# Twenty operations get another rank in a planned instruction order: linear attention, then a token-and-channel mixing block, on one core

## The chip, the cores and the metric

The kernel runs on one core of a Trainium2 chip. The metric is device time in microseconds (us): 360.75 us is the median of three runs of the kernel before, 360.08 the lowest and 361.04 the highest. The core has a matrix engine (TensorE, "PE" in the profile, with "PEld" for its weight loads), a vector engine (VectorE, "DVE"), a scalar engine (ScalarE, "ACT"), GpSimd ("POOL") and SyncE ("SP"), which issues most transfers. TensorE writes into PSUM, which has eight banks.

## The reference

Eight batches, eight heads, 576 rows, head size 64; the model width is 8 x 64 = 512 and the hidden width 2048.

```python
kv  = einsum('bhsd,bhse->bhde', k, v)            # no softmax: k and v are multiplied first
out = einsum('bhsd,bhde->bhse', q, kv)
out = out / sqrt(mean(out*out, -1) + 1e-6) * g_norm
x   = out as [batch, 576, 512]
a1  = alpha1 * x + beta1
u   = x + lam * einsum('ts,bsd->btd', w_tok, a1)  # mixes tokens
a2  = alpha2 * u + beta2
y   = u + lam * (relu(a2 @ w_ch1) @ w_ch2)        # mixes channels, two layers
```

## The kernel before

The kernel is written as a list of operations. Each call `P.op(engine, cost, function, r=..., w=...)` adds one: the engine that runs it (or a choice of two), a cost estimated in microseconds, what it reads and writes, and a function that emits its instructions. An operation has a number, `idx`, its place in that list. One operation can be many instructions: the product of line 893 for four chunks is 64 matmul instructions in the trace.

Work goes batch by batch, in chunks of 128 rows; chunks 0 to 3 cover rows 0 to 511, and "the tail" is the last 64 rows. For batch 0 the parts are these: the product k'v (line 694); q transposed by TensorE (line 723, two pairs of heads for each half of the heads, and line 737 for the tail); q times kv (line 893); its square on ACT (line 927), a sum on VectorE (line 929), a root (line 932) and a reciprocal (line 935), and the scaling (line 948); w_tok transposed (line 1452, five groups, and line 1466 for the tail columns), with ACT or VectorE copying each group out of PSUM, and summed (line 1488); token mixing (line 1134 for batch 0, line 1057 for batch 1, line 1088 for the tails of both batches), and the VectorE add of its result (lines 1151, 1070 and 1096); a transpose of u (line 1169) with a copy that scales it (lines 1178 and 1179); the first layer (lines 1235 and 1247 for the first four groups, 1220 for the others, sixteen groups `fj` of 128 hidden channels) with relu on ACT (line 1210); the second layer (line 1311), sixteen parts of four matmuls for batch 0, part n of chunk c adding hidden channels 4n to 4n+3 of sixteen, with a VectorE add (line 1321) after the last part of a chunk.

While batch 0 is in its layers, batch 1 is prepared: q is split into a high and a low half-precision part (copies that the trace shows at lines 564 and 565, subtraction at line 649), transposed by TensorE (line 672), multiplied by kv (line 881, with 459 for the second matmul of each pair), squared and scaled as before. Casts of the first-layer weights (trace lines 564 and 565) and scaling of the second-layer weights (line 1543) also run there.

The order on each engine is not the order of the list. `schedule` plays the program through in microseconds of its own: whenever an engine is free, it takes the operation of lowest rank `pri` that is ready, which means that what it needs is done and that a PSUM bank is free for its result. TensorE looks at the first sixteen operations of its queue. While the first layer of batch 0 has not begun and nothing is ready for TensorE, a filler matmul on zeros (line 1624) is put in. The result is a fixed order for each engine, written into the program with semaphores.

`plan` sets the ranks. It takes the operations on which the first layer and second layer of batch 0 and the first group of batch 1 depend, gives each a latest start worked backwards from due times, runs `schedule` eight times, and keeps the ranks of the best. A rank is about a planned start in microseconds, minus 1000. Operations that none of those need, such as everything later in batch 2 and onward, keep their number in the list as rank. The function `shake` adds random numbers to ranks for each seed, and the call passes no seeds:

```python
        for seed in seeds:
            kept_pri = shake(kept_pri, seed)
        run(kept_pri)
        ...
        P.plan(due, 8, ())
```

Of the kernel before, what the change touches and what calls it, by code (L numbers as in the profile page):

```python
# [2 lines left out]

# [46 lines left out]
class Prog:  # L50
# [72 lines left out]
                o.pri = -1000.0 - way  # L123
        return rank

    def plan(self, due, rounds, seeds):

        kept = [(o, o.eng, o.cost, set(o.deps)) for o in self.ops]
        tiles = {t: list(t.ops) for o in self.ops for t in o.tiles}
        ahead = sorted(self.hasten(due), key=lambda o: o.idx)  # L130
        movable = [o for o in ahead if o.eng != "SP"]

        def run(pri):
            self.ops[:] = [o for o, *_ in kept]
            for o, eng, cost, deps in kept:
                o.eng, o.cost, o.deps = eng, cost, set(deps)
                o.start = o.end = None
            for t, ops in tiles.items():
                t.bank, t.ops = None, list(ops)
            self.warm[3].bank, self.warm[3].ops = None, []  # L140
            self.lastw.pop(self.warm[3], None)
            for o in movable:
                o.pri = pri[o]
            for o in self.first:
                o.pri = -3000.0
            self.schedule()
            return max(o.end for o in self.ops)

        def backward():
            late, free, users = {}, {}, {}  # L150
            for o in ahead:
                for y in o.deps:
                    users.setdefault(y, []).append(o)
            base = max(o.start - d for o, d in due.items())
            for o, d in due.items():
                late[o] = base + d
            for o in sorted(ahead, key=lambda o: -o.end):
                if o in late:
                    continue
                by = min([late[u] for u in users.get(o, ()) if u in late] or [base])  # L160
                by -= o.end - o.start - o.cost
                if o.lat is None:
                    by = min(by, free.get(o.eng, 1e9))
                late[o] = by - o.cost
                if o.lat is None:
                    free[o.eng] = late[o]
            return {o: late[o] - 1000.0 for o in movable}

        def shake(pri, seed):
            rnd = random.Random(seed)  # L170
            share, by = (0.02, 0.1, 0.3)[seed % 3], (1.0, 3.0)[seed % 2]
            return {o: pri[o] + (rnd.gauss(0.0, by) if rnd.random() < share else 0.0)
                    for o in movable}

        pri = {o: o.pri for o in movable}
        best, kept_pri = None, None
        for i in range(rounds):
            last = run(pri)
            if best is None or last < best - 1e-6:
                best, kept_pri = last, pri  # L180
            pri = backward()
        for seed in seeds:
            kept_pri = shake(kept_pri, seed)
        run(kept_pri)

    def schedule(self):
        queues = {}
# [277 lines left out]
def bass_transnormer_attn__then__resmlp_affine_kernel(  # L465
# [15 lines left out]
    with ExitStack() as stack:  # L481
        P = Prog(nc, stack)
# [1016 lines left out]
        def run(gens):  # L1499
            for gen in gens:  # L1500
                for f in gen:
                    f()
# [47 lines left out]
        due = {}  # L1550
# [74 lines left out]
                            start=True, stop=True)  # L1625
        P.warm = (next(iter(due)), warm, ["wz"], P.ptile(1))
        P.first = [wz_op]
        P.plan(due, 8, ())
        P.synchronize()
        P.emit()  # L1630

# [27 lines left out]
```

## Time and profile before

| | |
|---|---|
| median of three runs | 360.75 us (360.08 to 361.04) |
| span of the profiled execution | 357.9 us |
| the profiled execution's own time | not listed beside the span; the median is 2.85 us above it |
| TensorE busy | 348.7 us, 97% |
| VectorE busy | 236.6 us, 66% |
| ScalarE busy | 158.9 us, 44% |
| GpSimd busy | 20.2 us, 6% |
| moved by DMA | 60.17 MB, 168 GB/s on average |

A timeline row gives the start, the length of a merged run of instructions, the engine, the line, what was written from what, and in brackets the idle time of the engine just before, with what ended it. In the view by stretch, "PE busy (x)" is the busy time of TensorE in that stretch with the number of its instructions. The span counts from the first instruction to the last; the runs' time also has what lies around it.

### The profile page before, as it was taken

Reading aid. Unit: us, or ns where it says so; the run is one execution under the profiler, and the core shown is the slowest. Engines: PE = TensorE matmul, PEld = TensorE weight load, DVE = VectorE, ACT = ScalarE, POOL = GpSimd, SP = SyncE. Lnnn points to the kernel's source line nnn. Section 1 sums busy time; section 2 is a strip of 40 time slices with the busy share of each in tenths; the row PEclk is TensorE's granted clock in tenths of the full one; section 3 lists DMA queues with packets and bytes.
Section 4 is the critical chain, followed back from the end, with each engine's and each line's share of the span. In section 5 each row is a group of like instructions: output and inputs, shape, how many; then the busy total and the mean of one; then the engine's idle time right before and its main releaser. Section 6 shows DMA issues by size and latency. Waiting matters only on the chain.

```text
span 357.9 us, 7888 instructions
## 1 busy us (share of the span) xinstructions
PE 348.7 (97%) x3570; PEld 204.3 (57%) x3387; DVE 236.6 (66%) x347; ACT 158.9 (44%) x270; POOL 20.2 (6%) x29
## 2 busy tenths in 40 slices
PE   8999999999999999999999999999999999999996
PEld 7778554477644544467644554457654554457644
DVE  3478899778993389947884388956885369920021
ACT  2556983068800494028810396017930185007600
POOL 4152004300000000000000000000000000000000
PEclk9999999999999999999999999999999999999999
DMA  8999999499156930599256840486036400240022
GB/s 280 350 363 377 406 408 371 173 178 338 59 134 188 291 141 3 117 186 336 100 117 181 268 185 2 101 178 194 3 83 153 116 6 0 55 132 6 2 59 88
DMA packets 79897, 60.17 MB, mean 168 GB/s; under 512 B 53037, under 2 KB 63541, under 8 KB 79736
## 3 DMA queue, kind: packets, MB, share of 16 engines
q1 hardware_dynamic: 79840, 59.67, 54.7%
q8 instruction: 27, 0.44, 0.5%
q14 instruction: 6, 0.05, 0.0%
q10 hardware_dynamic: 24, 0.01, 0.0%
HBM read 38.82 MB, written 9.44 MB: 135 GB/s over the span
## 4 chain that ended last, share of the span: by engine, by line
PE 94%; ACT 4%; issue 1%; DVE 0%
PE ps L1311 34%; PE ps L1262 20%; PE ps L1220 13%; PE ps L1057 7%; PE ps L694 5%; PE ps L1624 2%; PE ps L881 2%; PE ps L459 2%; ACT ht L1210 2%; PE ps L1088 1%; PE ps L1134 1%; PE ps L723 1%; PE ps L1292 1%; PE ps L1169 1%; PE ps L1109 1%
## 5 line engine op out<-in xcount | busy, mean ns | idle before, releaser
L1311 PE MATMUL ps<-w,ht 128*128 128x512 bf16 x537 | 121.8, 379 | 2.2 <-issue 1.4
L1209 ACT ACTIVATE ht<-ps,hb 128x512 bf16<-128x512 f32 (+1 forms) x96 | 71.0, 740 | 43.1 <-PE ps L1262 31.9
L1311 PEld LDWEIGHTS ps<-w,ht 128*128 128x128 bf16 x560 | 53.5, 98 | 63.7 <-issue 2.0
L1262 PE MATMUL ps<-a2t,w 128*128 128x320 bf16 (+1 forms) x512 | 72.7, 299 | 0.0
L1262 PEld LDWEIGHTS ps<-a2t,w 128*128 128x128 bf16 x512 | 49.4, 98 | 20.4
L1220 PE MATMUL ps<-a2t,w 128*128 128x512 bf16 x231 | 53.1, 379 | 1.0 <-issue 0.7
L758 ACT ACTIVATE kvd<-ps 64x128 bf16<-64x128 f32 x24 | 6.5, 272 | 96.0 <-PE ps L694 95.9
L1321 DVE TENSOR_TENSOR xm<-ps,xm 128x512 f32<-128x512 f32 x31 | 20.8, 687 | 29.7 <-PE ps L1311 29.6
L1220 PEld LDWEIGHTS ps<-a2t,w 128*128 128x128 bf16 x240 | 22.7, 98 | 26.1 <-issue 0.5
L929 DVE TENSOR_REDUCE small<-sq 128x16 f32<-128x1024 f32 (+1 forms) x18 | 20.2, 1126 | 16.6 <-ACT sq L927 16.6
L1057 PE MATMUL ps<-rt,wt 128*128 128x512 bf16 x107 | 25.1, 379 | 0.3
L1210 ACT ACTIVATE ht<-ps 128x512 bf16<-128x512 f32 (+1 forms) x32 | 19.9, 665 | 1.3 <-DVE hb L565 0.6
L763 DVE TENSOR_TENSOR kvd<-ps,kvd 64x128 bf16<-64x128 f32 x24 | 6.9, 289 | 20.4 <-ACT kvd L758 20.0
L948 DVE TENSOR_TENSOR xm<-ps,small 128x1024 f32<-128x1024 f32 x16 | 19.6, 1224 | 0.5
L1070 DVE TENSOR_TENSOR xm<-ps,xm 128x1024 f32<-128x1024 f32 x14 | 17.1, 1222 | 4.2 <-PE ps L1109 2.6
L927 ACT ACTIVATE sq<-ps 128x1024 f32<-128x1024 f32 (+1 forms) x18 | 17.0, 951 | 6.0 <-PE ps L893 4.0
L694 PEld LDWEIGHTS ps<-vf,kf 64*64 64x64 f32 x1008 | 16.0, 135 | 5.6 <-issue 4.4
L694 PE MATMUL ps<-vf,kf 64*64 64x64 f32 x1008 | 17.9, 221 | 0.6 <-ACT a2t L1178 0.6
L1057 PEld LDWEIGHTS ps<-rt,wt 128*128 128x128 bf16 x112 | 10.9, 98 | 12.9 <-issue 0.4
L1321 DVE TENSOR_TENSOR xtl<-ps,xtl 128x512 f32<-128x512 f32 x4 | 2.8, 692 | 21.2 <-PE ps L1311 21.1
L649 DVE TENSOR_TENSOR qs<-qf,qs 128x1024 bf16<-128x1024 f32 x14 | 16.7, 1215 | 0.1
L1076 DVE TENSOR_TENSOR a2b<-xm,a_bc 128x512 bf16<-128x512 f32 x24 | 15.5, 688 | 0.4
(130 smaller groups left out, 337.0 us busy)
## 6 DMA issues: line engine op xcount, KB each, us to landing
out_dram<-xm SPq DMA_DIRECT2D x31, 256.0 KB, 2.7
qf<-in_q_dram SPq DMA_DIRECT2D x7, 1024.0 KB, 6.8
kf<-in_k_dram SPq DMA_DIRECT2D x6, 1152.0 KB
vf<-in_v_dram SPq DMA_DIRECT2D x6, 1152.0 KB, 10.0
stg<-in_moe_w_ch_dram SPq DMA_DIRECT2D x3, 1024.0 KB, 13.7
kf<-in_moe_w_ch_dram SPq DMA_DIRECT2D x2, 1024.0 KB
kf<-in_k_dram SPq DMA_DIRECT2D x2, 576.0 KB, 5.1
vf<-in_v_dram SPq DMA_DIRECT2D x2, 576.0 KB, 6.3
```

Of the source, the lines that this page charges most:

```text
L694: m = e.matmul(t.ap(slice(64 * x, 64 * x + 64))[:, y, 0:64], nine(kf, b, a)[r, x, c, :], nine(vf, b, a)[r, x, c, :], start=(c == 0), stop= ...
L927: P.op("ACT", act_us(64 * m), lambda e: e.activation(split(sqv) if b == 0 else sqv, raw(), ACT.Square), r=[t], w=[("sq", sqs)])
L929: P.op("DVE", dve_us(64 * m), lambda e: e.tensor_reduce(out=smv, in_=sqv.rearrange("p (h d) -> p h d", h=m), axis=AX.X, op=ALU.add), r=[(" ...
L948: P.op("DVE", dve_us(64 * m), lambda e: e.tensor_tensor(out=x3, in0=raw() if b == 0 else split(raw()), in1=inv, op=ALU.mult), r=[t, ("sm", ...
L1057: m = e.matmul(t.ap()[:, i, :], tok_w(sc, c), rsrc(b, sc), start=(sc == 0), stop=(sc == 4))
L1070: P.op("DVE", dve_us(512 * n), lambda e: e.tensor_tensor(out=x, in0=t.ap(rows) if n > 1 else t.flat(rows), in1=x, op=ALU.add), r=[t] + xk, ...
L1209: o = P.op("ACT", act_us(n) + 0.07 * (b > 1), lambda e: e.activation(dst, src(), ACT.Relu, bias=hb[:, fj:fj + 1]) if b > 1 else e.activati ...
L1210: dst, src(), ACT.Relu, bias=hb[:, fj:fj + 1]) if b > 1 else e.activation(
L1220: m = e.matmul(t.flat(), w, a2t[:, dj, 0:512], start=(dj == 0), stop=(dj == 3))
L1262: m = e.matmul(t.ap()[:, i, 0:n], w1[:, dj, 128 * fj:128 * fj + 128], a2t[:, dj, 320 * i:320 * i + n], start=(dj == 0), stop=(dj == 3))
L1311: m = e.matmul(t.flat(), ht[:, fj, 128 * c:128 * c + 128], w2[:, fj, :], start=(fj == 0), stop=(fj == 15))
L1321: P.op("DVE", dve_us(512), lambda e: e.tensor_tensor(out=x, in0=t.flat(), in1=x, op=ALU.add), r=[t] + keys, w=keys)
```

## The change

The third argument of `plan` is now a table of moves, from an operation's number to a value in microseconds that is added to its rank before the last call of `schedule`. A negative value ranks the operation earlier, a positive one later. `shake` goes, which was never called.

```diff
-    def plan(self, due, rounds, seeds):
+    def plan(self, due, rounds, moves):
...
-        for seed in seeds:
-            kept_pri = shake(kept_pri, seed)
-        run(kept_pri)
+        run({o: kept_pri[o] + moves.get(o.idx, 0.0) for o in movable})
...
-        P.plan(due, 8, ())
+        P.plan(due, 8, {
+            52: -8.5, 56: -7.8, 68: 2.6, 129: 7.7, 154: 4, 158: 13.5, 159: 5.2, 162: 11.6,
+            169: 3.2, 204: -2.1, 205: -10.7, 237: 13.4, 246: 2.9, 254: 13.8, 258: 7, 273: 20,
+            276: 8.5, 278: 8.6, 283: 88.2, 298: -5.6})
```

Counting the calls of `P.op` gives what the numbers stand for:

| number | move | operation (line in the trace, engine) |
|---|---|---|
| 52 | -8.5 | batch 0, q of the second half of the heads transposed, first pair (723, TensorE) |
| 56 | -7.8 | batch 0, q tail of the second half transposed (737, TensorE) |
| 68 | +2.6 | tail columns of w_tok transposed (1466, TensorE) |
| 129 | +7.7 | cast of a piece of the first-layer weights (564 or 565) |
| 154 | +4 | batch 1, high part of q, chunks 0 and 1 (564 or 565) |
| 158, 159 | +13.5, +5.2 | batch 1, high part and low part of q, tail (564 or 565; 649) |
| 162 | +11.6 | batch 1, q of chunks 2 and 3, first half of the heads, transposed (672, TensorE) |
| 169 | +3.2 | batch 1, copy of the transposed q, chunks 2 and 3, second half (564 or 565) |
| 204 | -2.1 | batch 1, q times kv, chunks 0 and 1 (881, TensorE) |
| 205 | -10.7 | its square (927, ACT) |
| 237 | +13.4 | batch 1, reciprocal for the tail (1006, VectorE) |
| 246, 254, 258 | +2.9, +13.8, +7 | batch 0, first layer, groups 6, 10 and 12 (1220, TensorE) |
| 273 | +20 | batch 1, token mixing of chunk 2 (1057, TensorE) |
| 276 | +8.5 | token mixing of the tails of batches 0 and 1 (1088, TensorE) |
| 278, 283 | +8.6, +88.2 | batch 0, second layer, chunk 0 part 0 and chunk 1 part 1 (1311, TensorE) |
| 298 | -5.6 | batch 1, first transpose of u (1169, TensorE) |

Since `schedule` plays all engines through together, an operation that is not in the table can change its place too.

More of the change, by code (lines that the diff above doesn't have):

```diff
@@ L1 @@
-import random
 from contextlib import ExitStack
@@ L167, in backward @@
             return {o: late[o] - 1000.0 for o in movable}
[L169 to L173, printed above, removed]
         pri = {o: o.pri for o in movable}
```

## The prediction

> **What bounds the kernel now.** I read the page's busy table first, then the clock row, then busy time by stretch, then the PE timeline of the first 77 us, because every moved operation lies in there.
>
> ```profile
> span 357.9 us, 7888 instructions
> PE 348.7 (97%) x3570; PEld 204.3 (57%) x3387; DVE 236.6 (66%) x347; ACT 158.9 (44%) x270; POOL 20.2 (6%) x29
> ...
> PEclk9999999999999999999999999999999999999999
> ```
>
> ```profile
> core 0: us, PE busy (x) PEld busy (x) DVE busy (x) ACT busy (x) POOL busy (x), PEclk, DMA share, GB/s
> 6.00:26.00 20.00, 19.23 (x419) 15.14 (x421) 12.56 (x24) 10.17 (x22) 5.30 (x8) 1.00 1.06 359
> 26.00:52.00 26.00, 25.84 (x305) 17.32 (x276) 22.46 (x31) 20.81 (x35) 3.44 (x5) 1.00 1.06 396
> 52.00:71.50 19.50, 19.39 (x96) 8.72 (x95) 16.94 (x21) 4.73 (x8) 7.66 (x5) 1.00 0.79 285
> 71.50:77.00 5.50, 4.93 (x166) 4.35 (x165) 5.28 (x8) 3.66 (x9) 0.00 (x0) 1.00 0.80 180
> ```
>
> TensorE is busy 97% of the span at a granted clock of 1.00, so the time is the sum of what TensorE does plus its holes. The change keeps the same operations, so the useful matmuls cannot get shorter; only holes can go or come. The stretches have holes of 20.00 − 19.23 = 0.77, 26.00 − 25.84 = 0.16, 19.50 − 19.39 = 0.11 and 5.50 − 4.93 = 0.57 us: 1.61 us in all. Some of that is not real: a matmul record can be missing. Two more holes are hidden inside the busy time, namely filler matmuls of zeros (line 1624) that the planner puts in wherever TensorE has nothing ready before the first layer of batch 0 begins.
>
> ```profile
> 14.10 1.97 PE L723 MATMUL ps<-ident,qf 128*64 128x128 f32 x32
> 16.00 0.33 PE L737 MATMUL ps<-ident,qft 64*128 64x64 f32 x2
> 16.11 0.60 ACT L564 ACTIVATE qt<-ps 128x512 f32<-128x512 f32 x1
> 16.26 0.55 PEld L1624 LDWEIGHTS ps<-a2b 128*128 128x128 bf16 x4
> 16.37 0.29 DVE L565 COPY qt<-ps 128x128 f32<-128x128 f32 x1
> 17.23 0.44 PE L893 MATMUL ps<-kvd,qt 64*64 64x64 f32 x7
> 18.06 1.17 PE L893 MATMUL ps<-kvd,qt 64*64 64x64 f32 x65 [0.39 <-issue]
> 19.16 0.75 PE L1466 MATMUL ps<-ident,ht 64*128 64x64 f32 x5
> 19.84 1.23 PE L1452 MATMUL ps<-ident,ht 128*128 128x128 f32 x8
> 20.62 1.18 ACT L564 ACTIVATE wt<-ps 128x512 bf16<-128x512 f32 x3
> 20.78 0.43 PEld L1624 LDWEIGHTS ps<-a2b 128*128 128x128 bf16 x3
> 21.55 1.55 PE L1452 MATMUL ps<-ident,ht 128*128 128x128 f32 x12
> 22.22 1.55 ACT L564 ACTIVATE wt<-ps 128x512 bf16<-128x512 f32 x3
> 22.93 1.47 PE L1134 MATMUL ps<-rt,wt 128*128 128x256 bf16 x12
> 24.24 1.70 PE L1488 MATMUL ps<-wt,sel 128*128 128x512 bf16 x10
> ```
>
> The weight loads count the fillers: four from 16.26 and three from 20.78. Between them stands a hole of 0.39 us that no engine ended ("issue"), before line 893. The last hole is the only one with a named releaser:
>
> ```profile
> 52.11 12.90 PE L1311 MATMUL ps<-w,ht 128*128 128x512 bf16 x58
> 64.94 1.05 PE L1088 MATMUL ps<-rt,wt 128*64 128x512 bf16 x8
> ...
> 69.39 1.03 PE L1311 MATMUL ps<-w,ht 128*128 128x512 bf16 x4
> 70.25 1.03 PE L1057 MATMUL ps<-rt,wt 128*128 128x512 bf16 x4
> ...
> 71.33 0.60 PE L1169 MATMUL ps<-ident,xtl 128*128 128x128 f32 x4
> 71.53 1.23 DVE L1070 TENSOR_TENSOR xm<-ps,xm 128x1024 f32<-128x1024 f32 x1
> 71.64 1.50 ACT L1178 ACTIVATE a2t<-ps,ab 128x128 bf16<-128x128 f32 x4 [9.18 <-PE ps L1169]
> 72.50 1.28 PE L694 MATMUL ps<-vf,kf 64*64 64x64 f32 x72 [0.57 <-ACT a2t L1178]
> 73.80 0.69 DVE L1321 TENSOR_TENSOR xm<-ps,xm 128x512 f32<-128x512 f32 x1
> ```
>
> The kv product of batch 2 (line 694) needs two neighbouring banks of PSUM and has to wait until ACT empties some of the four small transposes (line 1169). One wide matmul lasts (64.94 − 52.11) / 60 = 0.214 us; sixty stand for fifteen second-layer parts of four, of which two records are missing. So the three fillers at 20.78 are worth 0.64 us and the four at 16.26 are worth 0.86.
>
> **The ceiling.** The moved operations come at 14 us and later. What they can at most take away is 0.86 + 0.39 + 0.64 + 0.57 = 2.46 us. After 77 us nothing is moved by hand, and the order there starts from the same state, somewhat earlier.
>
> **The change, part by part.** *Operations 52 and 56.* Operation 52 (line 723, q of the second half) cannot start before its data have landed. In the trace it already follows the kv product without a hole, so its new rank changes nothing: 0. Operation 56 (line 737) now goes before the second pair of line 723 instead of behind it. That delays this pair by 0.27 us (16.27 − 16.00) and its copy on ACT from 16.71 to about 16.98, while the small product that needs the tail can run where fillers ran. The large product of line 893, however, starts at 18.06 behind the "issue" hole, more than a microsecond behind that copy. I read the hole as instructions that had not yet been fetched, since all 16 DMA engines are busy (share 1.06) and no semaphore is named. Then fewer fillers ahead of it only lengthen the hole: 0, between −0.86 − 0.39 (hole and fillers go) and +0.27 (the delayed pair reaches the product). I take 0, as the row nearest to it is the one at 18.06. If the hole is a wait that moves with the product instead, at least its 0.39 us goes as well, and the forecast below becomes 359.1; that is part of the rival in which more goes. The Trainium skill, page "Runtime: NRT & Kernel Launch", section "Instruction fetch mechanics", speaks for this second reading: it holds that fetching the next block is mostly hidden behind the issue of the current one. This trace shows the hole, without a cause.
>
> *Operation 68* (line 1466, tails of the w_tok transposes) goes behind three of the five transposes of line 1452. In the trace it is first; then come two groups of line 1452, and then TensorE runs out: three fillers until ACT's copies (from 20.62) return a bank. With the tail later, the two banks of the small product of line 893 come back sooner as well, because its chain on ACT and DVE started earlier. So the fillers go: −0.64. The bounds are 0 (the banks return no sooner, since ACT's three copies run back to back until 21.80) and −0.64. Whatever is late next is line 1488 at 24.24, which needs ACT's last copy of w_tok; that ends at 22.22 + 1.55 = 23.77, 0.47 us ahead of it, and token mixing of chunks that are ready (line 1134) can fill the rest, so I let all of the gain pass.
>
> *Operations 129, 154, 158, 159, 162, 169, 204, 205 and the first-layer groups 246, 254, 258.* They sit in a stretch with 0.16 us of holes, so there is nothing to win there. Here is what it could lose:
>
> ```profile
> 34.74 0.63 ACT L564 ACTIVATE qs<-qft 64x512 bf16<-64x512 f32 x1
> ...
> 38.74 6.21 PE L1220 MATMUL ps<-a2t,w 128*128 128x512 bf16 x27
> ...
> 41.40 1.04 ACT L564 ACTIVATE qt<-ps 128x1024 bf16<-128x1024 bf16 x1
> 42.31 3.57 ACT L1210 ACTIVATE ht<-ps 128x512 bf16<-128x512 f32 x7
> 44.79 0.19 PE L881 MATMUL ps<-kvd,qt 128*128 128x64 bf16 x1
> 45.92 1.02 ACT L927 ACTIVATE sq<-ps 128x1024 f32<-128x1024 f32 x1
> ```
>
> The first whole group of line 1220 starts at 38.74 and takes four matmuls, so it ends near 39.60; its relu runs at 42.31. ACT is 2.7 us behind, and banks cover that. Each relu takes 3.57 / 7 = 0.51 us against 0.86 us for a group, so ACT then gains 0.35 us a group. The change puts the q·kv product (204) about three groups earlier and its square (205, 1.02 us) before relus that it used to follow, and pushes the cast 158 (0.63 us) and the transposes 162 out of the way. With 158 gone from 34.74, ACT is 0.63 us ahead when 205 comes: net +0.39 us behind. I count 0 with bounds 0 and +1.65 (1.02 + 0.63, if 158 falls among the relus and no bank covers it).
>
> *Operations 237, 273, 276, 278, 283, 298.* 237 only lets the other VectorE work of batch 1 go first; token mixing needs both, and that chain has slack:
>
> ```profile
> 51.88 2.49 DVE L929 TENSOR_REDUCE small<-sq 128x16 f32<-128x1024 f32 x2
> ...
> 60.64 1.23 DVE L954 TENSOR_TENSOR rt<-xm,e1g_bc 128x1024 bf16<-128x1024 f32 x1
> ```
>
> Its last piece ends at 61.87, and token mixing starts only at 64.94: 3.07 us. The moves 276 and 273 let the last second-layer part of batch 0 (now the row at 69.39, after chunk 2 of token mixing) go ahead of chunk 2. In the old order its bank stays occupied until VectorE's add at 73.80 has run; in the new one the part is finished early enough for the add to run in VectorE's free time before token mixing. 283 holds back three parts of chunk 1 (its own, and two that continue the same sum), 3 × 0.86 = 2.57 us that fill TensorE when nothing else is ready. So the hole at 71.93 closes: −0.57, bounds −0.57 and +0.5. The upper bound is the VectorE add of line 1070 (1.23 us) uncovered in place of the 0.57 us hole, if 283's parts were used up before, less about 0.15 us of work that still covers it.
>
> The sum: 0 − 0.64 + 0 − 0.57 = −1.21 us on a span of 357.9. The profiled execution's own total is not listed; the median of the runs, 360.75, stands 2.85 us over the span, and I keep that: 356.7 + 2.85 = 359.5.
>
> **Rivals.** *One or none of the two holes closes.* For it: the 20.78 fillers end when ACT's copies do, and ACT's work there is unchanged; the late hole depends on which two banks are free. Against it: both holes are waits for a bank, and the order is what decides that. Result: between 360.75 − 0.64 = 360.1 and 360.75; I set 360.4.
>
> *More goes than that:* the issue hole (359.1) or the fillers at 16.26 too, 360.75 − 2.46 = 358.3 at the best.
>
> *Slower: ACT becomes the bound at 42 us.* 204's two banks are taken at about 41.5 (three groups, 2.6 us, earlier) instead of 44.79 and are given back only after VectorE's chain from 51.88 on, so the first layer lives on six banks. ACT's backlog of 2.7 + 1.02 = 3.7 us is 4.3 groups, plus the group being written, plus the bank of the copy at 41.40, plus two: 8.3. It decides from the eighth bank, so this is on the edge. Then TensorE follows ACT, and the 0.64 won before is swallowed: +1.65, which with the late hole closed or open is 361.8 to 362.4; I set 362.1. Against it: removing 0.63 us at 34.74 pulls the count to 7.6. The Trainium skill, page "TensorE: Matmul & The Clock Gate", states that the queues of ScalarE and VectorE are strictly first in, first out; by that a square whose product is late would hold every relu behind it as well, which no row here shows.
>
> **How the numbers follow.** About 0.3% (1.08 us) is what a measurement of this kernel can tell from no change. Both holes closed: 0.40, 359.5. More than both: 0.07. Both count as faster, 0.47. One or none, or small losses against small gains: 0.38, within 0.3%. ACT and the banks: 0.15, slower. The range from 358.5 to 361.5 leaves out the slower case and the far end of the best one; the forecast's own range is 359.1 to 360.1, as both signs of the edge at 42 us are small in it.
>
> **What would show it.** Right: no filler weight loads between 19 and 23 us, line 1134 starting near 22.3 instead of 22.93, the large product of line 893 still near 18.06, and no hole with an ACT releaser ahead of line 694 near 71 us. The row of four matmuls of line 1311 between two chunks of line 1057 is gone. Wrong: holes on TensorE between 41 and 47 us before line 1220 with ACT as releaser; fillers that only moved; a wait for line 1070 before line 1169; or differences that arise after 77 us, which this reasoning holds to be none.

## The result, and the profile after

The kernel after takes 361.56 us in the median of 15 runs (360.66 to 362.45); the kernel before, on the same chip, takes 360.19 us in 15 runs (359.54 to 361.21). The ratio is 1.0038, with a 95% interval of 1.0028 to 1.0048: slower by 1.37 us, where the prediction had 1.2 us faster. In the code of the kernel after, every line below the deleted function stands 9 lines higher than before: 685, 884, 1079, 1160, 1211 and 1302 are the old 694, 893, 1088, 1169, 1220 and 1311. The kernels of the experiments keep the old numbers.

Lines of the page of the kernel after: the span, the busy table, the clock and two of the DMA queues.

```profile
span 359.7 us, 7936 instructions
...
PE 353.3 (98%) x3611; PEld 204.4 (57%) x3387; DVE 236.6 (66%) x351; ACT 157.0 (44%) x266; POOL 21.9 (6%) x29
...
PEclk9999999999999999999999999999999999999999
...
q8 instruction: 27, 0.44, 0.5%
```

The span has grown by 359.7 − 357.9 = 1.8 us at the same clock. TensorE's busy time must not be compared: the kernel before has 3570 matmul records and the kernel after 3611, so 41 are missing in the trace of before, which has the same matmuls. What can be compared is the start of the same step in both traces. The last line is of a kind that the prediction did not look at: 27 packets of instructions, 0.44 MB, come in over a queue of their own.

Busy time by stretch, kernel after (the last row has no counterpart in the prediction):

```profile
core 0: us, PE busy (x) PEld busy (x) DVE busy (x) ACT busy (x) POOL busy (x), PEclk, DMA share, GB/s
6.00:26.00 20.00, 19.74 (x414) 14.55 (x412) 12.22 (x25) 9.63 (x20) 4.35 (x6) 1.00 1.05 352
...
52.00:71.50 19.50, 19.20 (x96) 8.70 (x95) 19.36 (x23) 5.72 (x11) 7.73 (x5) 1.00 0.97 345
71.50:77.00 5.50, 5.50 (x103) 4.27 (x102) 3.10 (x5) 3.18 (x6) 0.00 (x0) 1.00 1.09 182
...
195.00:210.00 15.00, 13.59 (x251) 7.93 (x217) 4.66 (x12) 4.95 (x11) 0.00 (x0) 1.00 0.94 295
```

The hole of 0.57 us between 71.5 and 77 us is gone, as forecast. One of 15.00 − 13.59 = 1.41 us has come between 195 and 210 us, 130 us behind the last moved operation. The matmul timeline of the kernel after around the first q·kv products of batch 0:

```profile
16.85 0.60 PE L1615 MATMUL ps<-a2b 128*128 128x512 bf16 x2
17.39 0.45 PE L884 MATMUL ps<-kvd,qt 64*64 64x64 f32 x8
17.77 0.39 PE L1615 MATMUL ps<-a2b 128*128 128x512 bf16 x1
18.42 0.59 PE L1615 MATMUL ps<-a2b 128*128 128x512 bf16 x2 [0.26 <-issue]
18.94 1.16 PE L884 MATMUL ps<-kvd,qt 64*64 64x64 f32 x64
...
21.58 0.38 PE L1615 MATMUL ps<-a2b 128*128 128x512 bf16 x1
...
23.59 0.38 PE L1615 MATMUL ps<-a2b 128*128 128x512 bf16 x1
23.81 1.47 PE L1125 MATMUL ps<-rt,wt 128*128 128x256 bf16 x12
```

Line 1615 is the filler. There are seven fillers between the transposed q tail and token mixing, as before; they have only moved: five stand ahead of the large product (before: four), two behind it (before: three). Three now stand between the small product (17.39) and the large one (18.94), which starts 0.88 us later than the 18.06 of before, 0.37 us of which is there already in the first product (12.11 against 11.74 us), before any moved operation. From the large product to token mixing it is 23.81 − 18.94 = 4.87 us, and before it was 22.93 − 18.06 = 4.87 us.

One row of the late stretch, matmul timeline of the kernel after:

```profile
66.62 1.05 PE L1079 MATMUL ps<-rt,wt 128*64 128x512 bf16 x8 [0.30 <-DVE xm L1312]
```

The start of batch 4's first layer in the matmul timeline, first of the kernel before, then of the kernel after:

```profile
201.69 0.81 PE L1311 MATMUL ps<-w,ht 128*128 128x512 bf16 x3 [0.16 <-issue]
202.34 0.81 PE L1220 MATMUL ps<-a2t,w 128*128 128x512 bf16 x3
203.37 1.24 PE L1220 MATMUL ps<-a2t,w 128*128 128x512 bf16 x5 [0.21 <-issue]
```

```profile
202.03 1.04 PE L1302 MATMUL ps<-w,ht 128*128 128x512 bf16 x4
204.48 1.89 PE L1211 MATMUL ps<-a2t,w 128*128 128x512 bf16 x8 [1.41 <-DVE kvd L758]
```

The 0.16 us in the first row of before is a missing record and not a hole, as the kernel after has four matmuls there. A bracket counts from the modelled end of the last matmul; measured by the usual spacing of starts (0.21 to 0.22 us), the delay is 0.16 to 0.18 us longer: 0.38 us before and 1.59 us after.

Taken together, the same step starts later than before by 0.37 us at 12 us, 0.87 at 19 us, 0.57 from 77 to 202 us (hole at 72 gone, a new one of 0.30 at 66.62), and 1.76 us from 204 us to the end. The largest single part, 1.19 us, arises where nothing was moved.

The name in the last row (DVE kvd) is not the cause. With the same order and 24 instructions fewer (below), the same matmul starts at 202.74 us, and the copy that the name stands for (line 767 in the numbers of before) only at 203.22 us, so it does not depend on that copy. That leaves the instruction itself as what was late; the next section asks why.

### The profile page after: what moved, and what is told of

The parts are those of the page before. It is cut to its first block, busy times and chain, and to the rows that moved or that the text cites. A ratio compares the mean times of both kernels' runs of the same rounds, so it can differ in the third digit from the quotient of the medians.

```text
span 359.7 us, 7936 instructions
## 1 busy us (share of the span) xinstructions
PE 353.3 (98%) x3611; PEld 204.4 (57%) x3387; DVE 236.6 (66%) x351; ACT 157.0 (44%) x266; POOL 21.9 (6%) x29
## 4 chain that ended last, share of the span: by engine, by line
PE 88%; DVE 9%; issue 1%; ACT 1%
PE ps L1302 31%; PE ps L1253 19%; PE ps L1211 12%; PE ps L1048 6%; PE ps L685 5%; DVE w L1534 3%; PE ps L1615 2%; PE ps L872 2%; PE ps L450 2%; PE ps L1079 1%; PE ps L1125 1%; PE ps L714 1%; PE ps L1283 1%; PE ps L1100 1%; DVE qs L640 1%
## 5 line engine op out<-in xcount | busy, mean ns | idle before, releaser
L1302 PE MATMUL ps<-w,ht 128*128 128x512 bf16 x560 | 125.9, 379 | 0.0
L1211 PE MATMUL ps<-a2t,w 128*128 128x512 bf16 x240 | 55.0, 379 | 1.4 <-DVE kvd L758 1.4
L555 ACT ACTIVATE qs<-qf 128x1024 bf16<-128x1024 f32 x13 | 13.5, 1048 | 5.8 <-DMA qf<-in_q_dram 5.8
```

What stands on the lines that cost most here:

```text
L1211: m = e.matmul(t.flat(), w, a2t[:, dj, 0:512], start=(dj == 0), stop=(dj == 3))
L1302: m = e.matmul(t.flat(), ht[:, fj, 128 * c:128 * c + 128], w2[:, fj, :], start=(fj == 0), stop=(fj == 15))
```

## A reading of the holes that no engine ends

TensorE does not hold its whole instruction list from the start; parts of it come in while it runs. The 27 packets of the instruction queue carry 16,384 bytes each (0.44 MB in all). TensorE's compiled list has 7,056 instructions before and 7,062 after, of 64 bytes, so a packet holds a block of 256 instructions. The 6 extra ones are waits on semaphores (58 against 52), which the other order needs. The holes marked "issue" sit where one block of 256 ends: the one at 18.06 us behind position 707 of the list, the one at 203.37 behind position 4547, and 4547 − 707 = 15 × 256. Each ends 1.2 to 1.5 us after a packet of 16,384 bytes has come in.

Theory A: TensorE runs out of fetched instructions there and stands still until the next block is in. Just ahead of the second place come the two halves of batch 5's kv product (line 694, 144 instructions in 1.2 us each), which use up a block faster than the next one comes. With 6 more instructions ahead of it, the block ends right at the start of batch 4's first layer and not three matmuls (0.65 us) later. Theory B: the order itself costs the time, by waits on other engines. All runs below have 12 executions beside the kernel before on the same chip, except for the runs of the operations 129 to 258 alone and of operation 56 alone, which have 6; the medians of before are 360.19, 360.12 and 359.97 us in the three groups.

## Experiments on the block of instructions

**Six more instructions in the order of before.** One filler of 512 columns is issued as four of 128, the same matmul time.

```diff
+        fillers = [o for o in P.sequence if o.eng == "PE" and o.ins == 2 and o.idx >= P.listed]
+        for o in fillers[43:44]:
+            o.fn = lambda e: [warm(e, P.warm[3], 128) for _ in range(4)][-1]
```

> The order of before, but one filler of 512 columns ahead of the first product is issued as four of 128, so that TensorE's list has six instructions more ahead of everything else, as many as the changed kernel has in batch 4, at no time of its own (the fillers only pass the wait for the first data). Theory A (the changed kernel lost most of its time where TensorE waits for the next 16 KB block of its instructions, and six instructions more moved the end of a block onto the start of batch 4's first layer): a hole of 0.8 to 1.4 us before line 1220 near 203 us, and 0.6 to 1.2 us over before. Theory B (the new order of the first 85 us costs the time by itself): as before, within 0.2 us. Theory C (batch 4's transposed input comes late because of the transfers' order): as before, since no transfer is moved.

Measured: 360.83 us (359.29 to 361.40), ratio 1.0019 [1.0004, 1.0035]. Its matmul timeline at batch 4:

```profile
201.13 1.04 PE L1311 MATMUL ps<-w,ht 128*128 128x512 bf16 x4
204.04 1.89 PE L1220 MATMUL ps<-a2t,w 128*128 128x512 bf16 x8 [1.87 <-DVE xtl L1321]
```

No operation is moved, and the hole of the kernel after is there, at the same matmul. Up to 202 us this run is 0.34 us ahead of before (in this execution the hole near 18 us did not occur), from 204 us on 1.32 us behind: 1.66 us in the two traces, 0.64 us in the medians, from six instructions. So the hole, the largest single part of the loss between the two traces, needs no change of the order. In the medians it is worth less: 0.64 of the 1.37 us, with an interval from about 0.1 to 1.3 us.

**The order of after, 24 instructions fewer.** Sixteen of the first fillers become four of 512 columns.

```diff
+        for i, o in enumerate(fillers[:16]):
+            o.fn = (lambda e: warm(e, P.warm[3], 512)) if i % 4 == 0 else (lambda e: None)
```

> The changed kernel's order; sixteen of the first fillers are issued as four of 512 columns in the same time, so that every later block of TensorE's instructions ends 24 instructions further on in the work. Theory A: no hole near 203 us (1.2 us less than the changed kernel), and the two fillers and the product near 18 us no longer both stand behind the block's arrival (0.5 us less): about 359.8, within 0.3 us of before. Theory B: as the changed kernel, 1.3 us over before. Theory C: as the changed kernel.

Measured: 360.21 us (359.60 to 361.58), ratio 1.001 [0.9995, 1.0024], 1.35 us below the kernel after. Its matmul timeline at batch 4:

```profile
201.86 1.04 PE L1311 MATMUL ps<-w,ht 128*128 128x512 bf16 x4
202.74 1.89 PE L1220 MATMUL ps<-a2t,w 128*128 128x512 bf16 x8
```

The hole is gone with all twenty moves in place. The block now ends 12 matmuls later; by then the packet is in.

**The order of before, also 24 instructions fewer**, by the same edit:

> The order of before with the same sixteen fillers as four wide ones. Theory A: the small hole near 203 us (0.16 us) goes and some 24 instructions of the product at 18 us run ahead of the block's arrival (0.2 us): 0.2 to 0.4 us under before. Theories B and C: as before, within 0.2 us.

Measured: 360.24 us (358.77 to 361.30), ratio 1.0007 [0.9992, 1.0022]; there is no hole at batch 4's first layer, but one in the q·kv product behind it, where the block now ends (0.50 us in the bracket, 0.66 us by the starts): the shift has moved the hole and not taken it away, and nothing is won. (This profiled execution began 1.44 us late, with its first data, so its offsets say less.)

The experiments further down give the theory a sharper test, as each has another number of instructions ahead of batch 4. Position 4547, counted from 0, is the last one of its block. "Ahead" is how many positions before 4547 the first weight load of batch 4's first layer stands in the compiled list (negative: behind it); with weight load and matmul in turn, that says how many matmuls should run before the hole. Packet times are from the DMA records of each trace:

| kernel | ahead | matmuls of the first layer before the hole | packet ends | TensorE resumes | behind the packet |
|---|---|---|---|---|---|
| before | 6 | 3 | 202.03 | 203.37 | 1.34 |
| 237 to 298 (the late moves) alone | 6 | 3 | 201.72 | 203.22 | 1.50 |
| 129 to 258 alone | 5 | 3 | 204.24 | 205.68 | 1.44 |
| 68 alone | 4 | 2 | 202.06 | 203.43 | 1.37 |
| 52, 56 and 68 alone | 4 | 2 | 202.49 | 203.84 | 1.35 |
| 129 to 298 | 2 | 1 | 202.81 | 204.07 | 1.26 |
| after | 0 | 0 | 203.10 | 204.48 | 1.38 |
| six more | 0 | 0 | 202.55 | 204.04 | 1.49 |
| 56 alone | −4 | 0; the last matmul of line 1311 waits too | 204.91 | 206.13 | 1.22 |
| before, nine fillers out | 24 | 8, and 5 of the q·kv product | 202.45 | 203.81 | 1.36 |
| before, 24 fewer | 30 | 8, and 9 of the q·kv product | 204.59 | 205.92 | 1.33 |
| late moves, nine fillers out | 24 | 8, and 5 of the q·kv product | 202.21 | 203.66 | 1.45 |
| after, nine fillers out | 18 | no hole | 202.26 | | |
| after, 24 fewer | 24 | no hole | 203.00 | | |

In the nine kernels where the block ends in or just ahead of the first layer, the number of matmuls before the hole is the one that the position gives; in three more it comes later, behind the first two groups of the layer. In all twelve the instruction at position 4547 runs before the hole, whatever it is, and the one behind it is the first late one. It is not a wait on an operation: the same step runs before the hole in one kernel and behind it in another. In the last two kernels TensorE reaches the end of the block over 1.6 us behind the packet, and there is no hole. How long the hole is depends on when the packet comes, and this differs between executions; the latency of a packet itself (0.9 to 1.1 us here, 1.33 in the one from 15.28 to 16.61 us of before) is part of that. Theory A holds for this place.

## Experiments on the moves

**Only 52, 56 and 68**:

```diff
+        P.moves = {52: -8.5, 56: -7.8, 68: 2.6}
```

> The changed ranks of operations 52, 56 and 68 alone. Theory A: the large product of line 893 near 18.9 us instead of 18.1, since two fillers now stand behind the arrival of a block (0.5 us); no gain from 68; in batch 4 the list is two instructions longer, 0.2 us or so: 0.5 to 0.9 us over before, with the hole of 0.57 us near 72 us still there. Theory B, as the prediction had it (56 neutral, 68 takes three fillers away): 0 to 0.64 us under before.

Measured: 360.80 us (360.12 to 362.08), ratio 1.0029 [1.0016, 1.0043]. In its matmul timeline the fillers stand where they stand in the kernel after:

```profile
17.73 0.45 PE L893 MATMUL ps<-kvd,qt 64*64 64x64 f32 x8
18.11 0.82 PE L1624 MATMUL ps<-a2b 128*128 128x512 bf16 x3
18.86 1.16 PE L893 MATMUL ps<-kvd,qt 64*64 64x64 f32 x64
```

From the first kv product of line 694 (13.68 us) to token mixing (23.72) it takes 10.04 us. In the order of before it takes 10.03 us (12.90 to 22.93) with the hole of 18.06 us, and 9.42 us without it (13.29 to 22.71, late moves alone, below). So the three moves cost 0.62 us, as much as the hole that this execution does not have. The fillers are instructions in the fixed order: the large product cannot start before them, whether its data are there or not.

**Only 68**, the move on which half of the forecast gain rested:

```diff
+        P.moves = {68: 2.6}
```

> Only operation 68 gets another rank. Theory: the fillers at 20.78 move behind the first transposes and before the small product of line 893 that follows, their number in the list stays at 55, and line 1134 starts as late after the large product as before (4.87 us): 360.1 to 360.4. By the prediction's step: no fillers in the 5 us after the large product and line 1134 0.64 us earlier, 359.5.

Measured: 360.09 us (359.74 to 361.65), ratio 1.0004 [0.999, 1.0019]. Its matmul timeline:

```profile
17.97 1.38 PE L893 MATMUL ps<-kvd,qt 64*64 64x64 f32 x72
19.28 1.72 PE L1452 MATMUL ps<-ident,ht 128*128 128x128 f32 x12
20.84 0.81 PE L1624 MATMUL ps<-a2b 128*128 128x512 bf16 x3
21.58 0.75 PE L1466 MATMUL ps<-ident,ht 64*128 64x64 f32 x5
...
23.28 1.47 PE L1134 MATMUL ps<-rt,wt 128*128 128x256 bf16 x12
```

From product to token mixing it is 23.28 − 17.97 = 5.31 us. In the order of before it is 22.93 − 17.23 = 5.70 us with the hole, and 5.09 us in the executions that do not have it (17.62 to 22.71 with the late moves alone, 17.50 to 22.59 with six more instructions). So the move costs 0.22 us when alone, which the median, 0.12 us above before, cannot tell from nothing. The three fillers remain, now behind three groups of line 1452 and not behind two. This step of the prediction fails.

**Only 56**:

```diff
+        P.moves = {56: -7.8}
```

> Only operation 56 gets another rank. Theory: its small product goes ahead, the fillers that stood there now stand between small and large product of line 893, and the large product starts 0.3 to 0.5 us later relative to the first product than in a run without a hole near 18 us; 360.3 to 360.8. By the prediction's step: same start of the large product, 360.1.

Measured: 362.80 us (361.35 to 364.96), ratio 1.0075 [1.0045, 1.0105]: far outside what either reading expected, and the worst of all. Two fences of its matmul timeline:

```profile
13.99 0.33 PE L737 MATMUL ps<-ident,qft 64*128 64x64 f32 x2
14.26 0.82 PE L1624 MATMUL ps<-a2b 128*128 128x512 bf16 x3
15.01 1.97 PE L723 MATMUL ps<-ident,qf 128*64 128x128 f32 x32
16.91 0.44 PE L893 MATMUL ps<-kvd,qt 64*64 64x64 f32 x7
18.87 0.21 PE L893 MATMUL ps<-kvd,qt 64*64 64x64 f32 x1 [1.52 <-issue]
19.02 1.25 PE L1624 MATMUL ps<-a2b 128*128 128x512 bf16 x5
20.20 1.16 PE L893 MATMUL ps<-kvd,qt 64*64 64x64 f32 x64
```

```profile
203.70 0.82 PE L1311 MATMUL ps<-w,ht 128*128 128x512 bf16 x3
206.13 0.38 PE L1311 MATMUL ps<-w,ht 128*128 128x512 bf16 x1 [1.61 <-issue]
```

Without 52, the tail goes ahead of both pairs of line 723, not of the second alone. Three fillers and the tail delay both pairs by 1.02 us against the kv product before them (15.01 − 12.79 against 14.10 − 12.90), and five fillers come ahead of the large product. On top of that, both block ends cost their full price in this execution, 1.52 us behind position 707 and 1.61 us at batch 4. By the timelines, the move 52, which I had counted at nothing, keeps 56 from costing more: with it the tail goes ahead of the second pair alone. No run has 52 and 56 without 68, and this run's extra loss is also that of its block ends.

**Only 129 to 258** (the middle moves), the stretch with 0.16 us of holes:

```diff
+        P.moves = {129: 7.7, 154: 4, 158: 13.5, 159: 5.2, 162: 11.6, 169: 3.2,
+                   204: -2.1, 205: -10.7, 246: 2.9, 254: 13.8, 258: 7}
```

> Only the mid moves, 129 to 258, get another rank. Theory: they cost 0.3 to 0.8 us between 38 and 66 us by a hole before line 1088 (in the changed kernel 0.30 us, released by VectorE's xm), and the hole at 72 us stays; with a block end far from the start of batch 4's first layer 360.5 to 361.0, with a hole there 361 to 362. Rival (the mid moves are free, as predicted): step-by-step offset against before unchanged from 38 us to 72 us, 360.0 to 360.3.

Measured: 362.39 us (361.98 to 363.92), ratio 1.0072 [1.005, 1.0094]; more than I expected. The holes with a releaser in its matmul timeline between 30 and 74 us:

```profile
49.64 0.20 PE L881 MATMUL ps<-kvd,qt 128*128 128x64 bf16 x1 [0.62 <-DVE qt L565]
...
60.07 2.76 PE L1311 MATMUL ps<-w,ht 128*128 128x512 bf16 x12 [0.69 <-ACT ht L1210]
...
63.59 1.05 PE L1088 MATMUL ps<-rt,wt 128*64 128x512 bf16 x8 [0.75 <-DVE rt L954]
```

All three are new, and the old one of 0.57 us before line 694 is still there behind them. Between 24 and 77 us the same step goes from 0.38 us early to 2.10 us late; 2.06 us of that are these three waits. ACT and VectorE do become the bound, as the slower rival had it, but not where it said: not at 41 to 47 us on banks, but at 49.6 us on a copy of the transposed q behind weight scaling on VectorE, at 60 us on the relu of one of the last groups, which now runs at 58.35 us with too little second layer left ahead of it, and at 63.6 us on batch 1's scaled rows.

**Only 237 to 298** (the late moves):

```diff
+        P.moves = {237: 13.4, 273: 20, 276: 8.5, 278: 8.6, 283: 88.2, 298: -5.6}
```

> The changed ranks of operations 237, 273, 276, 278, 283 and 298 alone; TensorE's list has the same number of instructions ahead of batch 4 as before. Theory A (blocks of instructions): the hole of 0.57 us near 72 us goes, one of up to 0.3 us may come, nothing else changes: 0.2 to 0.6 us under before. Theory B (the new order costs by itself): the late moves are the ones that cost, 0.3 us or more over before.

Measured: 359.86 us (358.87 to 360.78), ratio 0.9987 [0.9967, 1.0007]. Two rows of its matmul timeline:

```profile
71.63 1.28 PE L694 MATMUL ps<-vf,kf 64*64 64x64 f32 x72
...
203.22 1.24 PE L1220 MATMUL ps<-a2t,w 128*128 128x512 bf16 x5 [0.85 <-issue]
```

The hole before line 694 is gone and no other takes its place: from 0.23 us ahead of before at 51 us to 0.87 us ahead at 72.5 us, a gain of 0.64 us where the prediction had 0.57. Then the block end at batch 4 takes 0.64 us back, 0.85 against 0.21 us, with the same position in the list: here only the time of TensorE's arrival and of the packet differ.

**129 to 298**, all but the first three:

```diff
+        P.moves = {...}      # the table of the change without 52, 56 and 68
```

> All moves but those of 52, 56 and 68. TensorE's list is four instructions longer ahead of batch 4. Theory A: near 18 us as before; the hole near 72 us closed as in the changed kernel (0.3 us less); near 203 us a hole larger by about 0.43 us (4 instructions of 0.108 us), more when the block is late: between 0.1 and 0.9 us over before. Theory B, with the cost in the reordered first layer (ACT and the banks between 41 and 47 us): a hole there, 1 us or more over before.

Measured: 361.17 us (360.84 to 362.12), ratio 1.0026 [1.0007, 1.0046]. Its matmul timeline:

```profile
66.02 1.05 PE L1088 MATMUL ps<-rt,wt 128*64 128x512 bf16 x8 [0.54 <-DVE xm L1321]
...
204.07 1.67 PE L1220 MATMUL ps<-a2t,w 128*128 128x512 bf16 x7 [1.38 <-issue]
```

With the late moves the waits at 60 and 63.6 us are gone, as the last group of the first layer runs at 55.38 us and not at 58.35, with a row of 31 matmuls of the second layer behind it; what stays is 0.54 us before the tails of token mixing. From 24 to 84 us it loses 0.17 us against before. The rest is the block end.

## Experiments that take the fillers and the block end away together

Nine of the ten last fillers (zeros, no part of the result) are left out, in three orders. This also makes the list 18 instructions shorter, so that the first layer of batch 4 has 18 to 24 positions left before the block ends.

```diff
+        for o in fillers[45:-1]:
+            o.fn = lambda e: None
```

**In the order of after:**

> The changed kernel without nine of the ten fillers that follow the first product; nothing else is left out, and TensorE's list is 18 instructions shorter from 24 us on. Theory A: the product of line 893 that stood behind fillers near 18.9 us begins when its block of instructions is there, 0.5 us or more earlier; no hole near 203 us (1.2 us): 359.6 to 360.1, 1.3 to 1.9 us under the changed kernel. Theory B: no more than 0.2 us under the changed kernel.

Measured: 359.77 us (359.23 to 360.13), ratio 0.999 [0.997, 1.0009]: 1.79 us below the kernel after. Rows of its matmul timeline with a named releaser:

```profile
49.44 0.20 PE L881 MATMUL ps<-kvd,qt 128*128 128x64 bf16 x1 [0.66 <-DVE qt L565]
...
66.21 1.05 PE L1088 MATMUL ps<-rt,wt 128*64 128x512 bf16 x8 [0.54 <-DVE xm L1321]
```

Token mixing starts at 22.32 us, 1.49 us earlier than in the kernel after, but at 86 us only 0.41 us of that is left: the waits on VectorE come up as soon as TensorE comes early. There is no hole at 202 us.

**In the order of before:**

> The order of before; nine of the ten fillers that stand behind the small product of line 893 are left out (zeros, not part of the result), so TensorE's list is 18 instructions shorter and its blocks end 18 instructions later in the work. Theory A (a block of instructions that ends at the start of batch 4's first layer costs up to 1.4 us; the late moves of 237, 273, 276, 278, 283, 298 bring 0.6 us; fillers themselves cost next to nothing): no hole over 0.3 us at 202 to 205 us, the hole of 0.57 us before line 694 near 72 us still there, median 359.6 to 360.2, so the 358.8 of the same shortening with the late moves is the late moves' 0.6 to 0.8 and more. Rival (the gain of that run came from the missing fillers): about 358.8 to 359.2 here as well.

Measured: 359.56 us (358.73 to 360.47), ratio 0.9988 [0.9973, 1.0002]. The median lies 0.04 us under the range that I gave, and well above that of the rival. Two rows of its matmul timeline:

```profile
71.69 1.28 PE L694 MATMUL ps<-vf,kf 64*64 64x64 f32 x72 [0.57 <-ACT a2t L1178]
...
201.74 1.89 PE L1220 MATMUL ps<-a2t,w 128*128 128x512 bf16 x8
```

The hole before line 694 is there, as expected; the one at the block end is 0.20 us by the starts (before: 0.38), in the q·kv product.

**In the order of before with the late moves:**

> The late moves alone, without nine of the ten fillers. Theory A: the late moves' 0.3 us, the small hole near 203 us (0.16 us), and up to 0.4 us near 18 us where the product runs some instructions ahead of the block: 359.3 to 359.9, the fastest of all so far. Theory B: as the late moves alone.

Measured: 358.80 us (358.39 to 360.68), ratio 0.9971 [0.9949, 0.9992], faster than both kernels. In its matmul timeline the hole before line 694 and the one in batch 4's first layer are gone:

```profile
71.64 1.28 PE L694 MATMUL ps<-vf,kf 64*64 64x64 f32 x72
...
201.56 1.89 PE L1220 MATMUL ps<-a2t,w 128*128 128x512 bf16 x8
```

These three have the block end at batch 4 nearly out of the way. The order of before takes 359.56 us, that of after 359.77, that with the late moves alone 358.80; by the ratios 0.9988, 0.999 and 0.9971, whose intervals overlap. With the traces beside them (0.64 us of gain at line 694), the reading is that the twenty moves by themselves do about nothing, that six of them bring 0.6 to 0.8 us, and that the fourteen others give it back. The medians alone do not show this. Nor are the earlier block ends out of the way: at position 451, inside the first q·kv product, 0.6 to 0.85 us pass between two weight loads in all three traces, and at 707 there is a hole of 0.68 us in the trace with the late moves alone.

## Why the prediction was wrong, point by point

- **The bound** was read rightly: TensorE at full clock, and only holes and fillers can move. The step compared across traces bears this out in every run.
- **"After 77 us nothing is moved by hand"**, so no difference should arise there: this is the step that failed most. Nothing is moved there, but six instructions were added ahead of it, and 1.19 of the 1.76 us arise at 203 us. The hole of 0.21 us at 203.37 us stood in the trace of before, with the same "issue" as the one at 18.06 us, outside the stretches that I read. I had read the hole at 18.06 us rightly as instructions not yet fetched, and did not ask where else a block would end and whether the change shifts it. The Trainium skill, page "Runtime: NRT & Kernel Launch", section "Instruction fetch mechanics", gives blocks of 16 KiB and 256 instructions, with which the packets agree, and holds the fetch to be mostly hidden; at this place it is not, and the delay by the starts is 0.2 to 2.05 us in the twelve kernels with a hole.
- **Operations 52 and 56, counted at 0**: with 68 they cost 0.62 us against the order of before without its hole, and 0.50 us between the two traces first compared. The working stopped at the transposes and the copy. It let the small product run "where fillers ran" without asking where the fillers would go: three went between small and large product. Fewer fillers ahead of the hole did not lengthen it; it went from 0.39 to 0.26 us and the fillers came behind it.
- **Operation 68, counted at −0.64**, gains nothing: 4.87 us from large product to token mixing before and after, 0.22 us lost when alone. The other bound that I gave, 0, because ACT's copies run back to back, was nearer. I took the other end on the argument that the small product's banks come back sooner; the run of 68 alone shows the same three fillers one group later. "Fillers that only moved" stood in the list of what would show it wrong.
- **The middle moves, counted at 0** with a bound of +1.65 us: alone they cost 2.5 us in the trace and 2.4 us in the median, beyond the bound. Middle and late moves together, from 24 to 86 us, run from 0.31 us gained (the kernel after, where TensorE comes late) over 0.17 lost (129 to 298) to 0.76 lost (without fillers, where it comes early): these waits on VectorE also take back what the early part wins. I sized ACT's queue at 42 us, and did not follow what waits on VectorE at 49 to 66 us, though it was busy for 16.94 of the 19.50 us from 52 us on.
- **The late moves, counted at −0.57**: right as a mechanism and in size, −0.64 us when alone. In the kernel after the hole at 72 us goes too, but 0.30 us comes at 66.62 us through the middle moves.
- **The sum**: forecast −1.21 us; in the two traces it is +0.50 (56 and its fillers), −0.30 (middle and late moves), +1.19 (the block end) and +0.37 us, which is there ahead of all moves: the first q·kv product, up to which nothing is moved, starts between 11.63 and 12.20 us in the traces of before and of the seven runs that change nothing but ranks. Without that last term the sum is +1.39 us, beside +1.37 us in the medians. That this fits so closely is luck, as the block end alone differs by 0.64 us between two traces with the same position in the list (0.21 and 0.85 us).
- **The forecast time, 359.5 us**, also rests on 2.85 us between span and run. In the kernel after it is 361.47 − 359.68 = 1.79 us, and 1.78 to 1.82 us in all profiled runs of the experiments. The 2.85 us came from setting the span beside the median of other executions; with 1.8 us the forecast span of 356.7 us would have been 358.5 us.
- **The rival "slower"**, at 361.8 to 362.4 us, came nearest to the 361.56 us, but by luck: the kernel after has no hole between 40 and 48 us, where that rival put its loss.

## What to carry to other kernels

An edit that changes the order also changes the number of instructions on an engine, by its semaphore waits if by nothing else, and with it where the blocks of its instruction list end. So look for holes marked "issue" over the whole span, not only where the edit is: behind a run of very short instructions such a hole can grow by a microsecond from six instructions. And a filler in a fixed order is an instruction like any other: when the work around it moves, follow the filler, since it may come to stand ahead of work that is ready.

## What the hardware showed that I had not expected

TensorE resumes 1.2 to 1.5 us after the packet of its next 256 instructions has arrived, in the twelve holes of the table and in four near 18 us (1.45 in before, 1.52 in after, 1.23 with 56 alone, 1.32 with the late moves and nine fillers out). Packet and wait together take 2.2 to 2.5 us at batch 4. The two products that go ahead of batch 4's first layer use 288 instructions in 2.4 us, so 256 of them take about 2.1 us (an estimate), less than packet and wait. At most block ends nothing shows: over the 14 traces, the first weight load of a block starts 1.2 us or more behind its packet, and under 2.5 us only at four of the block ends (positions 451, 707, 1987 and 4547), which all lie in or near runs of such short instructions. The name that the profile gives to such a hole can be that of another engine ("DVE kvd", "DVE xtl"), where that engine merely finished last. What sets the time at which a packet is requested and how long it takes, and so why the same position shows 0.21 us in one execution and 0.85 us in another, stays open: the packet that begins at 15.28 us in the trace of before begins between 14.70 and 16.34 us in the others, and no run separated the effect of the other transfers on it.
